# The eight-row sums of k and v: from a reduction on VectorE to three in-place additions on GpSimd

## Chip, core and metric

The kernel runs on one core of a Trainium2 chip. The metric is the device time of one execution in microseconds (us); the median of the executions is compared.

## What is computed

Attention over keys and values that are pooled by eight along the sequence, then two blocks of matrix products. The shapes are: batch 8, 8 heads, sequence 576, head size 64; 4608 tokens of width 512 afterwards.

```python
k_p = k.reshape(B, H, Sp, pool, D).mean(axis=3)      # pool = 8, Sp = 72
v_p = v.reshape(B, H, Sp, pool, D).mean(axis=3)
scores = scale * np.matmul(q, k_p.transpose(0, 1, 3, 2))
attn = softmax(scores)
x = np.matmul(attn, v_p)          # tokens x 512
h = ((x @ w1) * (x @ w2)) @ w3    # first block, width 1024
y = h @ w_out
r = np.maximum(y @ w_in, 0.0)     # second block, width 2048
out = (r * r) @ moe2_w_out
```

The change concerns the first two lines only: the sums over eight neighbouring rows of k and of v.

## The kernel before

The kernel computes w3 @ w_out once (the "fold": `fold`, L634, whose products are L754), so that the first block needs three products instead of four. While the fold runs, the attention of batches 0 and 1 runs between its steps; from about 119 us on the products of the first block take turns with the attention of the other batches, and from about 705 us on only the second block is left.

The weights come from DRAM as 64-bit words. For each 128x512 piece the SP queue loads `raw` (L130), ScalarE makes two passes (L136, L137), VectorE three (L145, L146 on `raw`, L148 on `w` or `wo`); TensorE transposes w3 (L696) or uses the piece as it is. A `raw` buffer is free again after L148, and only then can the next load of its ring start.

Per batch, k and v each are 576 pooled rows of 64 numbers, in five tiles: four of 128 rows and one of 64. A tile `kv` holds for each pooled row its eight source rows (128 x 8 x 64). `kv_parts` (L276 to L313) gives a list of steps: load a tile on the SP queue (L286, L288, L291), sum it (`total`, L296), and what follows. For k that is the copy of `kp` beside itself on GpSimd (L318, L319) and then TensorE's transposes (L353, L359). For v it is `cut`, which splits the sums into a high and a low part on VectorE (L328, L329), and `place`, which puts them in the operands `vl` and `vr` by 16 small DMAs on the SP queue (L334, L338). That makes ten sums per batch and 80 in all, each one instruction of VectorE.

Per tile of 128 queries the attention takes: scores on TensorE (L432), row maximum and its scaling on VectorE (L446, L447), exponentials on ScalarE (L449), the reciprocal sum on VectorE (L455, L456), then on GpSimd the product with it (L457) and two small copies (L461), then transposes on TensorE (L479, L484), a split into high and low parts on ScalarE and VectorE (L119, L120, L485, L487) and the product with v (L178, L497), whose result is split again (L510, L513). Five such tiles make one batch, 40 in all; they are called attention tiles here.

Each engine executes its instructions in one fixed order, and so does the SP queue. That order is settled when the program is built: the framework orders the instructions by its own estimate of when each can run, so that a change of one helper shifts neighbours as well.

Of the kernel before, what the change touches and what calls it, by code (L numbers as in the profile page):

```python
# [13 lines left out]
AX = mybir.AxisListType  # L14
# [3 lines left out]
POOL = 8  # L18
# [17 lines left out]
def attn_moe_moe2_kernel(  # L36
# [16 lines left out]
    nc = tc.nc  # L53
# [202 lines left out]
    def kv_rows(j):  # L256
        return P if j < NJ - 1 else JL
# [18 lines left out]
    def kv_parts(src, b, dst, last):  # L276

        flat = src[b].rearrange("h (s r) d -> (h s) r d", r=POOL)
        raws = {}

        def load(j):
            pool, tag = (raw_p, "raw") if b else (wW_p, "w")
            raws[j] = r = pool.tile([P, POOL, D], F32, tag=tag, name="kv")
            if src is k:
                n = kv_rows(j)
                nc.sync.dma_start(r[:n], flat[j * P:j * P + n])  # L286
            elif j < NP:
                nc.sync.dma_start(r, flat[j * 2 * SP:j * 2 * SP + P])  # L288
            else:
                for c in range(NP):  # L290
                    nc.sync.dma_start(  # L291
                        r[c * RM:(c + 1) * RM], flat[c * 2 * SP + P:(c + 1) * 2 * SP])

        def total(j):
            n = kv_rows(j)
            nc.vector.reduce_sum(  # L296
                dst(j)[:n], raws[j][:n].rearrange("p r d -> p d r"), axis=AX.X)

        def part(j):
            if j >= 2:  # L300
                total(j - 2)
            if j < NJ:
                load(j)

        if b == 0:
            fits = NJ if src is k else U1 - NJ
            for j in range(fits):
                load(j)
            rest = [lambda: [load(j) for j in range(fits, NJ)]]
            return rest + [(lambda j=j: total(j)) for j in range(NJ)] + last  # L310
        parts = [(lambda j=j: part(j)) for j in range(NJ + 2)] + last
        what = (src is k, b)
        back["kv"].extend((what, fn) for fn in parts)  # L313
# [1055 lines left out]
    for step in order:  # L1369
        if step[0] == "h":  # L1370
            _, p, u, n = step
# [61 lines left out]
```

## Time and profile before

| | us |
|---|---|
| median of 3 runs | 1554.29 |
| lowest and highest of them | 1553.34, 1557.86 |
| the profiled execution | 1549.5 |
| span of the profiled execution | 1547.7 |

The span runs from the first to the last instruction of the program. TensorE's matmuls are busy for 97% of it, VectorE for 64%, ScalarE for 50%, GpSimd for 5%. A share of the whole span is a mean over stages with different limits, so a table of stretches is read beside it, and the chain of work that ended last shows which engine each stretch hung on. A duration in such a row is that of the instruction as recorded, with what it waited inside the engine; a number in brackets is idle time ahead of it, and what ended that.

### The profile page before, as it was taken

To read this page: it belongs to the slowest core of one execution; us is meant where nothing else is said; L and a number is where in the kernel's file an instruction comes from. 1 tells how busy PE (TensorE), PEld (TensorE's weight loads), DVE (VectorE), ACT (ScalarE), POOL (GpSimd) and SP (SyncE) were. 2 spreads that over 40 slices of the span, in tenths; PEclk is the share of its full clock that TensorE was granted. 3 is DMA by queue.
4 is the path that set the end of the run, shared out by engine and by line. 5 is a ranking of instruction groups with operands and counts; after the bars stand their busy time and mean duration, and the time that the engine had idled before them with its cause. 6 is when DMAs were issued, how large, how long until landed. Compare 5 with 4: busy or idle time off the path is not lost.

```text
span 1547.7 us, 21838 instructions
## 1 busy us (share of the span) xinstructions
PE 1498.4 (97%) x6944; PEld 1204.2 (78%) x6944; DVE 989.7 (64%) x1778; ACT 780.7 (50%) x1905; POOL 82.1 (5%) x146
## 2 busy tenths in 40 slices
PE   5799999999999999999999999999999999999998
PEld 3457787877787787878887878887788778888888
DVE  7897675757565564767245477659665976576442
ACT  6766555444444444545134574456445644554431
POOL 1011111101010001100000000000000000000000
PEclk9999999999999999999999999999999999999999
DMA  9555656565564856667439777778777867776774
GB/s 297 185 155 153 169 169 179 161 186 154 171 189 137 261 151 178 186 222 242 117 127 310 202 204 231 206 207 230 222 207 207 231 195 206 207 222 191 212 223 150
DMA packets 300625, 303.86 MB, mean 196 GB/s; under 512 B 131296, under 2 KB 188640, under 8 KB 300512
## 3 DMA queue, kind: packets, MB, share of 16 engines
q1 hardware_dynamic: 295328, 293.04, 65.5%
q10 hardware_dynamic: 5184, 9.44, 1.7%
q8 instruction: 56, 0.92, 0.2%
q14 instruction: 57, 0.47, 0.1%
HBM read 243.27 MB, written 56.62 MB: 194 GB/s over the span
## 4 chain that ended last, share of the span: by engine, by line
PE 73%; DVE 12%; DMA 5%; ACT 4%; SPq 3%; issue 2%; DVEq 0%; ACTq 0%
PE ps_w L178 21%; PE o L1149 15%; PE acc L178 10%; PE ps_c L1062 5%; PE ps_d L1062 5%; PE ps_a L1062 5%; PE o L1209 3%; PE ps_h L178 3%; PE ps_b L1062 2%; DVE gs L1127 2%; PE ps_s L432 2%; DVE gt L120 2%; SPq L338 2%; DMA raw<-in_moe_w_dram 1%; PE ps_av L178 1%
## 5 line engine op out<-in xcount | busy, mean ns | idle before, releaser
L1149 PE MATMUL o<-gt,un 128*128 128x512 f32 x1344 | 330.9, 390 | 4.9 <-DVE gt L120 4.5
L1149 PEld LDWEIGHTS o<-gt,un 128*128 128x128 f32 x1344 | 251.6, 188 | 60.9 <-DVE gt L120 9.0
L120 DVE TENSOR_TENSOR gt<-gs,gt 128x512 fp32r<-128x512 f32 x240 | 164.2, 689 | 189.9 <-ACT gt L119 189.6
L178 PE MATMUL ps_w<-x,wt 128*128 128x512 f32 x960 | 249.9, 401 | 2.2 <-DVE x L513 1.1
L119 ACT CAST gt<-gs 128x512 fp32r<-128x512 f32 x240 | 148.5, 620 | 163.9 <-PE o L1149 111.2
L178 PE MATMUL acc<-gt,Wt 128*128 128x512 f32 x864 | 221.1, 397 | 1.3 <-ACT st L819 1.3
L178 PEld LDWEIGHTS ps_w<-x,wt 128*128 128x128 f32 x960 | 174.2, 189 | 39.1 <-DVE x L513 3.0
L178 PE MATMUL ps_w<-x,un 128*128 128x512 f32 x768 | 191.1, 396 | 2.1 <-DMA un<-u_w 2.1
L178 PEld LDWEIGHTS acc<-gt,Wt 128*128 128x128 f32 x864 | 158.8, 189 | 34.1 <-ACT st L819 1.8
L178 PEld LDWEIGHTS ps_w<-x,un 128*128 128x128 f32 x768 | 140.8, 188 | 30.8 <-ACT oq L872 1.8
L449 ACT ACTIVATE att<-ps_s,mx 128x72 f32<-128x72 f32 (+1 forms) x320 | 97.9, 321 | 64.0 <-DVE mx L447 59.7
L1069 ACT ACTIVATE r<-r 128x512 f32<-128x512 f32 x96 | 60.5, 631 | 113.0 <-DVE r L1099 112.3
L1062 PE MATMUL ps_a<-x2o,un 128*128 128x512 f32 x384 | 97.7, 390 | 1.6 <-ACT r L1069 1.6
L791 DVE TENSOR_TENSOR gf<-asb,ps_w 128x512 f32<-128x512 f32 x72 | 49.2, 684 | 77.5 <-PE ps_w L178 74.4
L1062 PE MATMUL ps_c<-x2o,un 128*128 128x512 f32 x384 | 97.9, 390 | 0.3 <-DVE u L1093 0.2
L1062 PE MATMUL ps_d<-x2o,un 128*128 128x512 f32 x384 | 97.5, 389 | 0.0
L1070 ACT ACTIVATE gs<-r 128x512 f32<-128x512 f32 x144 | 89.5, 628 | 1.6
L119 ACT CAST gt<-gf 128x512 fp32r<-128x512 f32 x72 | 44.8, 623 | 81.7 <-DVE gf L791 77.6
L1127 DVE TENSOR_TENSOR gs<-gs 128x512 f32<-128x512 f32 x128 | 83.9, 690 | 2.2 <-ACT gs L1070 0.9
L1062 PEld LDWEIGHTS ps_a<-x2o,un 128*128 128x128 f32 x384 | 72.0, 188 | 17.1 <-ACT r L1069 2.0
L1062 PEld LDWEIGHTS ps_c<-x2o,un 128*128 128x128 f32 x384 | 71.9, 188 | 16.3 <-DVE u L1093 1.5
L1062 PEld LDWEIGHTS ps_d<-x2o,un 128*128 128x128 f32 x384 | 72.1, 188 | 15.0
(109 smaller groups left out, 1957.3 us busy)
## 6 DMA issues: line engine op xcount, KB each, us to landing
un<-u_w SPq DMA_DIRECT2D x128, 256.0 KB
un<-u_A SPq DMA_DIRECT2D x128, 256.0 KB
un<-u_S SPq DMA_DIRECT2D x128, 256.0 KB
un<-u_oA SPq DMA_DIRECT2D x128, 256.0 KB
un<-u_oS SPq DMA_DIRECT2D x128, 256.0 KB
raw<-in_moe_w_dram SPq DMA_DIRECT2D x32, 512.0 KB
raw<-in_moe_w_out_dram SPq DMA_DIRECT2D x24, 512.0 KB
x2d<-st ACTq DMA_DIRECT2D x36, 256.0 KB
```

Of the source, the lines that this page charges most:

```text
L119: nc.scalar.copy(hi, src)
L120: (eng or nc.vector).tensor_sub(lo, src, f32(hi))
L178: (lambda a=a, b=b, i=i: nc.tensor.matmul(ps, a, b, start=first and i == 0, stop=last and i == n - 1))
L338: nc.sync.dma_start(f32(vr)[r0:r0 + RM, c, 1, :], vhl[c * RM:(c + 1) * RM, i // 2, NP, :])
L449: nc.scalar.activation(av[:, h0 + h], sv[:, h], ACTF.Exp, bias=mx[:n, h:h + 1], scale=scale, accum_out=sm[:n, h0 + h:h0 + h + 1])
L791: nc.vector.tensor_mul(gf, asb, pss[1])
L1062: nc.tensor.matmul(ps, l, r, start=first and j == 0, stop=j == len(todo) - 1, skip_group_check=True)
L1069: nc.scalar.activation(t, src, ACTF.Relu)
L1070: nc.scalar.activation(take(name), t, ACTF.Square)
L1127: nc.vector.tensor_sub(src, a, src)
L1149: nc.tensor.matmul(ob[x][o], l, r, start=u == 0 and m != 5 and j == 0, stop=u == NU - 1 and j == 2, skip_group_check=True)
L1209: nc.tensor.matmul(acc[o][:, y * PC:(y + 1) * PC], l, r, start=u == 0 and y == 0 and j == 0, stop=u == U2 - 1 and j == 2, skip_group_check ...
```

## The change

The sums of batch 0's k stay as they were. The other 75 sums are made on GpSimd, each by three additions: the upper four of the eight rows are added onto the lower four, in place in `kv` (128x256 numbers), then two onto two (128x128), then the last two into the destination (128x64). The second and third addition read what the one before wrote.

```diff
         def total(j):
             n = kv_rows(j)
-            nc.vector.reduce_sum(
-                dst(j)[:n], raws[j][:n].rearrange("p r d -> p d r"), axis=AX.X)
+            r = raws[j][:n]
+            if src is k and b == 0:
+                nc.vector.reduce_sum(dst(j)[:n], r.rearrange("p r d -> p d r"), axis=AX.X)
+                return
+            for w in (POOL // 2, POOL // 4):
+                nc.gpsimd.tensor_add(r[:, :w], r[:, :w], r[:, w:2 * w])
+            nc.gpsimd.tensor_add(dst(j)[:n], r[:, 0], r[:, 1])
```

Below this place all line numbers are larger by 5 in the changed kernel: L446 is L451 there, L457 is L462, and so on. Each row of the following lists is an instruction in its engine's order: line, operation, output, inputs, shape.

On GpSimd, before, from the copies of batch 0's k to the second attention tile:

```order
L318 COPY kp<-kp 128x4x64
L319 COPY kp<-kp 64x64
L457 TENSOR_TENSOR att_102<-att_102,sm 128x576
L461 COPY rem<-att_102 128x96 x2
L457 TENSOR_TENSOR att_103<-att_103,sm 128x576
L461 COPY rem<-att_103 128x96 x2
```

On GpSimd, with the change, the last of the three trees that stand between those copies and the first attention tile, and what follows it:

```order
L301 TENSOR_TENSOR kv<-kv 128x256
L301 TENSOR_TENSOR kv<-kv 128x128
L302 TENSOR_TENSOR vhl<-kv 128x64
L462 TENSOR_TENSOR att_102<-att_102,sm 128x576
L466 COPY rem<-att_102 128x96 x2
L462 TENSOR_TENSOR att_103<-att_103,sm 128x576
L466 COPY rem<-att_103 128x96 x2
```

Three trees of three additions for batch 0's v now stand ahead of the product of the first attention tile.

On VectorE, before, the last two sums of batch 0's v, up to its cut (L328, L329):

```order
L296 TENSOR_REDUCE vhl<-kv 128x64
L148 ISA w_419<-raw,w_419 128x1024
L145 TENSOR_SCALAR raw<-raw 128x512
L455 TENSOR_SCALAR sm<-sm 128x8
L146 SCALAR_TENSOR_TENSOR raw<-raw 128x2x256
L711 TENSOR_TENSOR wt<-w_419,wt 128x512
L148 ISA wo<-raw,wo 128x1024
L296 TENSOR_REDUCE vhl<-kv 64x64
L456 RECIPROCAL sm<-sm 128x8
L328 CAST vhl<-vhl 128x320
L329 TENSOR_TENSOR vhl<-vhl 128x320
```

On VectorE, with the change, the same place and what follows the cut (L333, L334 here):

```order
L716 TENSOR_TENSOR wt<-w_423,wt 128x512
L333 CAST vhl<-vhl 128x320
L334 TENSOR_TENSOR vhl<-vhl 128x320
L145 TENSOR_SCALAR raw<-raw 128x512
L146 SCALAR_TENSOR_TENSOR raw<-raw 128x2x256
L120 TENSOR_TENSOR Wt<-ps_w,Wt 128x512
L148 ISA w_457<-raw,w_457 128x1024
L145 TENSOR_SCALAR raw<-raw 128x512
L451 TENSOR_REDUCE mx<-ps_s 128x4
L146 SCALAR_TENSOR_TENSOR raw<-raw 128x2x256
```

The two sums are gone from ahead of the cut, and the row maxima of the third attention tile, which stood well ahead of the cut before (at L446, 13 rows above the first row of the list before), now come behind it, and with them that tile's reciprocal sum.

## Rows read from the trace of the kernel before

**Rows 1.** Page, part 1: engine, busy us (share of the span), instructions.

```profile
PE 1498.4 (97%) x6944; PEld 1204.2 (78%) x6944; DVE 989.7 (64%) x1778; ACT 780.7 (50%) x1905; POOL 82.1 (5%) x146
```

**Rows 2.** Stretches: length, busy us (instructions) by engine, TensorE clock, DMA share, GB/s.

```profile
17.00:70.00 53.00, 39.94 (x142) 20.12 (x141) 45.44 (x90) 39.19 (x108) 5.39 (x9) 0.98 0.64 206
70.00:119.00 49.00, 46.56 (x181) 26.10 (x180) 47.24 (x94) 33.53 (x98) 4.94 (x8) 0.96 0.59 186
119.00:705.00 586.00, 574.29 (x2762) 461.28 (x2763) 378.67 (x791) 291.27 (x982) 66.69 (x114) 1.00 0.62 179
705.00:1547.70 842.70, 831.40 (x3838) 691.64 (x3836) 509.19 (x792) 409.21 (x709) 1.61 (x3) 1.00 0.71 207
```

**Rows 3.** Chain that ended last, 17 to 66 us: start, length, what.

```profile
20.07 0.15 DVE vhl L296
20.22 0.79 issue
...
22.03 0.95 DVE vhl L296
...
45.55 0.07 DVE vhl L296
45.62 0.79 issue
...
49.37 0.93 DVE vhl L296
```

**Rows 4.** Timeline to 30 us: start, length, engine, line, what [idle before].

```profile
8.29 0.40 POOL L318 COPY kp<-kp 128x256 f32<-128x256 f32 x1 [4.85 <-DVE kp L296]
...
9.22 0.23 POOL L319 COPY kp<-kp 64x64 f32<-64x64 f32 x1 [0.54 <-DVE kp L296]
...
24.89 1.15 POOL L457 TENSOR_TENSOR att<-att,sm 128x576 f32<-128x576 f32 x1 [15.45 <-DVE mx L447]
```

**Rows 5.** Timeline, 81 to 98 us, GpSimd and VectorE.

```profile
81.83 1.15 POOL L457 TENSOR_TENSOR att<-att,sm 128x576 f32<-128x576 f32 x1 [27.71 <-DVE sm L456]
...
82.21 1.32 DVE L711 TENSOR_TENSOR wt<-w,wt 128x512 fp32r<-128x512 f32 x1
...
96.06 0.68 DVE L148 CUSTOM_DVE_ANT_0 w<-raw,w 128x1024 uint16<-128x1024 uint16 x1
96.19 0.80 POOL L318 COPY kp<-kp 128x256 f32<-128x256 f32 x1 [4.48 <-DVE kp L296]
```

**Rows 6.** Groups of VectorE, 17 to 119 us: busy, mean ns | idle before.

```profile
L146 DVE SCALAR_TENSOR_TENSOR raw<-raw 128x512 uint32<-128x512 uint32 x30 | 20.6, 687 | 0.3
L148 DVE CUSTOM_DVE_ANT_0 w<-raw,w 128x1024 uint16<-128x1024 uint16 x23 | 15.8, 686 | 0.2
L145 DVE TENSOR_SCALAR raw<-raw 128x512 uint32<-128x512 uint32 x30 | 12.7, 424 | 1.8 <-ACT w L137 1.4 <-ACT wo L137 0.3
L296 DVE TENSOR_REDUCE vhl<-kv 128x64 f32<-128x512 f32 (+1 forms) x10 | 10.2, 1032 | 0.0
L296 DVE TENSOR_REDUCE kp<-kv 128x64 f32<-128x512 f32 (+1 forms) x8 | 8.3, 1038 | 0.0
```

**Rows 7.** Timeline, 38 to 40 us, third attention tile on VectorE.

```profile
38.77 0.82 DVE L446 TENSOR_REDUCE mx<-ps_s 128x4 f32<-128x288 f32 x2
...
39.84 0.23 DVE L447 TENSOR_SCALAR mx<-mx 128x4 f32<-128x4 f32 x2
```

**Rows 8.** Timeline, 50 to 70 us, from the cut to the next loads.

```profile
50.72 3.94 SPq L334 DMA_DIRECT2D vl<-vhl  x4
...
54.77 7.56 SPq L338 DMA_DIRECT2D vr<-vhl  x12
...
62.43 4.82 SPq L130 DMA_DIRECT2D raw<-in_moe_w_dram  x8
...
69.54 0.80 PE L178 MATMUL ps_av<-aT,vl 128*128 128x256 f32 x2 [4.32 <-DVE x L513]
```

**Rows 9.** Line L457: who waited for it (us, times).

```profile
  PEld ps_t L479: 1.6, 2
```

## The prediction

> **What bounds the kernel now.** The page comes first: TensorE's matmuls are busy for 97% of the span, VectorE for 64%, GpSimd for 5% [rows 1]. That alone would say that work taken off VectorE is worth nothing, but the shares are means over stages. The table of stretches tells them apart [rows 2]. From 705 us on there is no sum of k or v any more, so nothing changes there. From 119 to 705 us TensorE is busy for 574.29 of 586 us; it idles 11.7 us and VectorE has a third of its time free, so this is TensorE's stretch. From 17 to 70 us it is the other way round: VectorE is busy for 45.44 of 53 us and TensorE for 39.94, so 13.1 us of TensorE's time are lost. From 70 to 119 us both are full: VectorE 47.24 of 49, TensorE 46.56, so only 2.4 us are lost there. The chain of waits agrees: up to 119 us it runs mostly through VectorE's passes over the weights and through the sums, after that through TensorE. Whatever the change gives, it gives in the first 119 us, and at most 15.5 us, the idle time of the two stretches.
>
> Of the sums, five lie between 17 and 70 us (batch 0's v), and 13 between 70 and 119 us (k and v of batch 1, three of batch 2's k): 18, at 1.03 us each [rows 6]. The other 57 that move lie in TensorE's stretch.
>
> **What is taken off VectorE.** A sum of 1.03 us stands in the chain with 0.86 to 0.95 us, since neighbours overlap by a little: four of the first five are in it, 0.15+0.79, 0.95, 0.07+0.79 and 0.93 (the "issue" behind a sum is its remainder) [rows 3]. The fifth doesn't stand in the chain, and I count it as nothing. So 3.7 us leave the chain before 50 us.
>
> **What GpSimd takes for it.** No row shows such an addition. The nearest is the product of an attention tile, also two inputs from SBUF: 1.15 us for 576 numbers per row [rows 4]. Two copies, 0.40 us for 256 numbers and 0.23 us for 64 [rows 4], make a fixed part of about 0.17 us. With it the product costs 1.7 ns a number, and a tree of 256+128+64 = 448 numbers is 3 x 0.17 + 0.76 = 1.27 us; without it, in proportion, 0.90 us. I take 1.27, because the copy of 64 numbers plainly doesn't shrink in proportion. 75 trees are 68 to 95 us on an engine that has 82 us of work in 1548 [rows 1]; GpSimd becomes no bound. Nor is the later end of a single sum a matter: GpSimd has idled 27.7 us before one product and 4.5 us before a copy [rows 5], so a tree begins when its load lands, while the sum waited its turn on VectorE.
>
> **What the trees do to VectorE.** This decides. While GpSimd made a product at 81.83 us, a subtraction of VectorE that reads two tiles from SBUF (L711) took 1.32 us [rows 5]; L146, of the same 128x512 and also with two inputs from SBUF, takes 0.69 us [rows 6]. In the other direction a copy of `kp` that started 0.13 us into VectorE's L148 took 0.80 us [rows 5], not 0.40 [rows 4]. The two engines exclude each other there. L145, L146 and L148, all on SBUF alone, fill 49.1 us from 17 to 119 us [rows 6], two thirds of the 74 us that VectorE is busy there without the sums (45.44 + 47.24 [rows 2] less 10.2 + 8.3); the rest reads mostly PSUM. So a tree can be paid for twice. Lower bound of its price to VectorE: nothing, where VectorE idles or reads PSUM. Upper bound: its whole 1.27 us, more than the sum cost. I take the part that grows with the numbers, 0.76 us, times two thirds to four fifths: 0.55 us. The fixed part, I assume, passes beside VectorE, as in the disturbed copy: VectorE ended at 96.74 us and the copy 0.25 us later, well under its 0.40. A tree is then a gain of 0.4 us of VectorE's time (bounds: -0.3 and +0.95).
>
> 17 to 70 us: 3.7 us leave the chain, five trees put back 5 x 0.55 = 2.8; gain 0.9 us. The order adds something. The row maxima of the third attention tile stood ahead of the cut of batch 0's v, 1.05 us [rows 7], and its reciprocal sum beside it; all of it now comes behind the cut. The cut matters: after it 16 small DMAs hold the SP queue from 50.72 to 62.33 us, eight loads of weights stand behind them from 62.43 us, and TensorE idles 4.32 us up to 69.54 us for want of them [rows 8]. A cut that is earlier moves all this forward, and what was moved behind it falls into the hole: 1.1 us. Together 2.0 us.
>
> 70 to 119 us: 13 trees free 13 x 0.4 = 5.2 us of VectorE, but TensorE can give back only its 2.4 us of idle time; I take half, 1.2 us.
>
> 119 to 705 us: 57 us leave VectorE, which isn't late there; the price is that a product waits behind trees on GpSimd, and a subtraction ahead of a matmul behind a tree. TensorE's weight loads have waited for the products 1.6 us in all [rows 9]. I take nothing, with 3 us to either side, as the framework also orders TensorE's steps anew all over this stretch.
>
> Sum: 2.0 + 1.2 + 0 = 3.2 us. The profiled execution took 1549.5 us and would take 1546.3. It lies 4.8 us under the median of the runs, 1554.29; against that, 1551 us.
>
> **The rivals.**
>
> *VectorE gains the whole sums* (faster). Between 17 and 119 us the trees fall beside L446, L513 and the other readers of PSUM, or into idle time. For it: GpSimd has nothing else to do, and the trees for batch 0's v can run while the weights' loads still fill the DMA queues. Then 3.7+1.1 us before 70 us and the 2.4 us after it: 1547 us; with the hole of 4.32 us closed as well, 1543 us. Against it: two thirds of VectorE's work collides.
>
> *The port costs more than the sums did* (slower). VectorE is full from 17 to 119 us, so every tree meets an instruction of its kind; if each addition stops it for its full length, a tree costs 1.27 us and saves 0.95: 18 x 0.32 = 5.8 us more, 1560 us. It decides as soon as more than three quarters of a tree's length is lost on VectorE. For it: L711 lost 0.63 us to the last 0.77 us of one product [rows 5, 6]. Against it: the fixed part, and that in the second stretch TensorE's queue is as full. The Trainium skill, in "SBUF — State Buffer", section "Who interferes with whom", states this rule: a GpSimd instruction that reads SBUF and a VectorE instruction with two SBUF inputs exclude each other for the whole instruction, whereas a reduction of VectorE never contends. By that rule the change swaps work that disturbs nobody for work that does; the trace agrees on L711 (1.32 us, where 0.69 us is usual) and shows no tree.
>
> *A tree that waits for its load holds an attention tile's product behind it on GpSimd* (slower). GpSimd takes its list in order, and TensorE takes its own in order as well. A product that is used at once is late by one tree, 1.27 us; eight such tiles out of 35 would cost 10 us, less the 3.2: 1561 us. Against it: only two waits of the weight loads on L457 in the whole trace, 1.6 us [rows 9], so nearly all products are early enough.
>
> **How the numbers follow.** A measurement of this kernel can tell 0.3%, 4.7 us, from no change. The forecast, a gain of 3 us that stays within that: 0.53. The first rival, in the part of it that passes 4.7 us: 0.31. The port: 0.10. The held products: 0.06. So faster 0.31, same 0.53, slower 0.16. The range goes from 1545 us, the first rival with a part of the hole closed, to 1559 us, just short of the two slower ones; some 0.1 is left out on either side.
>
> **What the profile of the changed kernel would show.** The busy time of VectorE falls by about 75 x 1.05 = 79 us, less 20 to 40 us by which L145, L146, L148, L711 and the subtractions that read SBUF become longer; their means from 17 to 119 us tell the price of the port directly (0.69 us before for L146 and L148). A tree takes 1.3 us in its three rows when undisturbed. The 16 small DMAs begin 1 to 3 us before 50.72 us, and the products of the first block begin that much earlier. If L146 and L148 keep 0.69 us, the first rival holds; if their means pass 0.9 us, the second. TensorE's idle time from 119 to 705 us stays near 11.7 us; if it grows beyond 17 us with L479 waiting for L462, it is the third. I would be wrong altogether if the second block's time changed.

## The result, and the profile after

The change is slower. The changed kernel takes 1571.24 us (median of 6 runs, 1567.93 to 1573.06), the kernel before 1553.39 us in the same comparison (6 runs, 1551.81 to 1557.86): a ratio of 1.0116, 95% interval 1.0099 to 1.0133, some 18 us. The forecast was 1551 us with a range of 1545 to 1559; the result lies 12 us above it. The profiled execution after has a span of 1571.0 us, where the one before had 1547.7: these two lie 23.3 us apart, 5 more than the medians, since the execution profiled before (1549.5 us) was quicker than any of the six and the one after (1572.78 us) slower than most.

Lines of the kernel after stand 5 further down (L457 became L462, L479 became L484); a tree is L301 twice and, for its last addition, L302.

First the page's part 1, as in [rows 1]: engine, busy us, share, instructions.

```profile
PE 1506.2 (96%) x6944; PEld 1209.7 (77%) x6944; DVE 935.0 (60%) x1703; ACT 783.3 (50%) x1905; POOL 213.0 (14%) x371
```

VectorE got what it was to get: it is busy for 54.7 us less. The span grew by 23.3 us all the same, and the row splits that: TensorE idles 15.5 us more (1571.0 - 1506.2 = 64.8 us, against 1547.7 - 1498.4 = 49.3), and is busy for 7.8 us more with the same 6944 matmuls. The second part is its clock. The mean granted clock fell from 0.996 to 0.990 (before, then after):

```profile
core 0: 1547.7 us, clock 0.996
...
core 0: 1571.0 us, clock 0.990
```

With two levels, 2.4 and 1.2 GHz, that is some 31 us at the lower one (2 x 0.010 x 1571), where before it was 12; 19 us more at half speed would be about 9 us of lost work if TensorE were busy throughout; for a part of that time it is idle.

Now the stretches of [rows 2], in the kernel after (length, then busy us and instructions of PE, PEld, DVE, ACT and POOL, TensorE's clock, DMA share, GB/s).

```profile
17.00:70.00 53.00, 41.18 (x142) 20.56 (x140) 43.32 (x82) 37.47 (x104) 16.14 (x24) 0.97 0.62 199
70.00:119.00 49.00, 39.58 (x146) 23.05 (x147) 41.12 (x80) 32.69 (x93) 30.71 (x46) 0.86 0.60 188
119.00:705.00 586.00, 566.59 (x2691) 453.03 (x2690) 314.63 (x695) 279.95 (x935) 158.84 (x284) 0.99 0.60 168
705.00:1571.00 866.00, 853.18 (x3946) 708.29 (x3944) 527.17 (x834) 426.21 (x764) 3.79 (x6) 1.00 0.72 209
```

From 70 to 119 us TensorE idles 9.4 us (2.4 before) and its clock is 0.86 (0.96 before). From 119 to 705 us it idles 19.4 us (11.7 before). GpSimd, which had 4.94 us of work from 70 to 119 us, has 30.71 there. After that nothing is added: what the kernel before does from 829 us on stands 23.2 us later here, right to the end.

What TensorE waits for is new too. This is, as in [rows 9], who waited for the product of an attention tile (line L462: us, times). TensorE's matmuls waited 9.4 us, where it was 0.5; its weight loads, which stand ahead of the same matmuls, waited 10.7 us in the same two gaps, where it was 1.6.

```profile
  PEld ps_t L484: 10.7, 2
  PE ps_t L484: 9.4, 2
  PEld ps_t L489: 0.7, 2
```

The 9.4 us are two gaps; of the 15.5 us by which TensorE's idle time grew, the other 6 have other causes. The first gap, in the timeline of GpSimd, VectorE and TensorE (start us, us, engine, line, what, [idle before <- whom it waited for]):

```profile
94.07 0.18 DVE L461 RECIPROCAL sm<-sm 64x8 f32<-64x8 f32 x1
...
79.86 1.37 POOL L301 TENSOR_TENSOR kv<-kv 128x256 f32<-128x256 f32 x2 [12.19 <-DMA kv<-in_k_dram]
...
91.18 2.35 POOL L323 COPY kp<-kp 128x256 f32<-128x256 f32 x1
93.50 1.25 POOL L301 TENSOR_TENSOR kv<-kv 64x256 f32<-64x256 f32 x2
94.83 0.77 POOL L302 TENSOR_TENSOR kp<-kv 64x64 f32<-64x64 f32 x1
95.67 0.58 POOL L324 COPY kp<-kp 64x64 f32<-64x64 f32 x1
96.21 1.32 POOL L301 TENSOR_TENSOR kv<-kv 128x256 f32<-128x256 f32 x2
97.61 0.65 POOL L302 TENSOR_TENSOR vhl<-kv 128x64 f32<-128x64 f32 x1
98.22 1.25 POOL L301 TENSOR_TENSOR kv<-kv 128x256 f32<-128x256 f32 x2
99.54 0.32 POOL L302 TENSOR_TENSOR vhl<-kv 128x64 f32<-128x64 f32 x1
99.82 1.14 POOL L462 TENSOR_TENSOR att<-att,sm 64x576 f32<-64x576 f32 x1
...
101.02 0.69 PE L484 MATMUL ps_t<-ident,att 64*128 64x64 f32 x4 [6.00 <-POOL att L462]
```

The reciprocal sum, the product's last input, is there at 94.25 us. GpSimd doesn't idle; it works through the rest of batch 1's k and two trees of its v, which stand ahead in its queue, and starts the product 5.56 us later.

The length of this train comes in part from VectorE's work on SBUF beside it. From 79.86 us, when the rows of batch 1's k land after 12.19 us of idle time, GpSimd works without a break up to the product at 99.82 us: seven trees, the product of tile 3 and the copies, 20 us in all. The copy of `kp` takes 2.35 us there, where it took 0.40 [rows 4]. At the undisturbed lengths (1.6 us from the start of a tree to what follows it at 98.22 us) the same work would take some 14 us, an estimate; the 6 us of difference are as much as the product's wait.

TensorE stands still for 6.00 us, and then runs slowly (the windows 95.00 to 101.10 and 101.10 to 107.00 us, columns as above; the clock is the third figure from the end):

```profile
95.00:101.10 6.10, 0.10 (x2) 0.09 (x2) 3.07 (x4) 1.23 (x3) 5.66 (x10) 0.78 0.94 233
101.10:107.00 5.90, 5.90 (x23) 3.98 (x24) 3.42 (x6) 3.29 (x9) 3.89 (x7) 0.64 0.43 141
```

The second gap begins with a wait for a load:

```profile
131.56 1.28 POOL L301 TENSOR_TENSOR kv<-kv 128x256 f32<-128x256 f32 x2 [11.90 <-DMA kv<-in_k_dram]
132.92 0.32 POOL L302 TENSOR_TENSOR kp<-kv 128x64 f32<-128x64 f32 x1
133.31 0.40 POOL L323 COPY kp<-kp 128x256 f32<-128x256 f32 x1
133.66 1.25 POOL L301 TENSOR_TENSOR kv<-kv 64x256 f32<-64x256 f32 x2
134.99 0.31 POOL L302 TENSOR_TENSOR kp<-kv 64x64 f32<-64x64 f32 x1
135.37 0.23 POOL L324 COPY kp<-kp 64x64 f32<-64x64 f32 x1
135.56 1.14 POOL L462 TENSOR_TENSOR att<-att,sm 128x576 f32<-128x576 f32 x1
...
136.75 1.12 PE L484 MATMUL ps_t<-ident,att 128*128 128x128 f32 x4 [3.42 <-POOL att L462]
```

GpSimd idles 11.90 us in front of a tree whose rows of k haven't landed, while a product whose inputs are there at 129.94 us, and the next one's at 133.17 us, stand behind it. Of the 5.62 us that the first of them waits, 1.6 are the rest of that load; the other 4 are the two trees and the copies behind it. Of the 40 products, four wait for 3.9 to 5.6 us (tiles 4, 5, 6 and 22, counted from 0); before, none waited over 0.5 us.

### The profile page after: what moved, and what is told of

Same layout as the page of the kernel before. It is cut to its first block, busy times and chain, and to the rows that moved or that the text cites. A ratio compares the mean times of both kernels' runs of the same rounds, so it can differ in the third digit from the quotient of the medians.

```text
span 1571.0 us, 22041 instructions
## 1 busy us (share of the span) xinstructions
PE 1506.2 (96%) x6944; PEld 1209.7 (77%) x6944; DVE 935.0 (60%) x1703; ACT 783.3 (50%) x1905; POOL 213.0 (14%) x371
## 4 chain that ended last, share of the span: by engine, by line
PE 72%; DVE 9%; DMA 6%; ACT 4%; SPq 3%; POOL 3%; issue 2%; DVEq 0%; POOLq 0%; ACTq 0%
PE ps_w L178 19%; PE o L1154 14%; PE acc L178 9%; PE ps_a L1067 5%; PE ps_c L1067 5%; PE ps_d L1067 5%; PE o L1214 3%; PE ps_h L178 3%; PE ps_w L759 2%; PE ps_b L1067 2%; DVE gs L1132 2%; PE ps_s L437 2%; DVE gt L120 2%; POOL kv L301 2%; DMA raw<-in_moe_w_out_dram 2%
## 5 line engine op out<-in xcount | busy, mean ns | idle before, releaser
L178 PE MATMUL ps_w<-x,wt 128*128 128x512 f32 x960 | 253.4, 405 | 5.6 <-ACT asb L792 3.8
L301 POOL TENSOR_TENSOR kv<-kv 128x256 f32<-128x256 f32 (+3 forms) x150 | 101.0, 674 | 94.4 <-DMA kv<-in_v_dram 48.6
L796 DVE TENSOR_TENSOR gf<-asb,ps_w 128x512 f32<-128x512 f32 x72 | 49.3, 685 | 98.7 <-PE ps_w L178 93.3
L462 POOL TENSOR_TENSOR att<-att,sm 128x576 f32<-128x576 f32 (+1 forms) x40 | 48.8, 1219 | 346.6 <-DVE sm L461 196.0
```

The costliest lines, as they stand in the source:

```text
L178: (lambda a=a, b=b, i=i: nc.tensor.matmul(ps, a, b, start=first and i == 0, stop=last and i == n - 1))
L301: nc.gpsimd.tensor_add(r[:, :w], r[:, :w], r[:, w:2 * w])
L462: nc.gpsimd.tensor_mul(av, av, sm[:n].unsqueeze(2).to_broadcast([n, H, SP]))
L796: nc.vector.tensor_mul(gf, asb, pss[1])
```

## The experiments

The theories: **Q**, finished products wait on GpSimd behind trees. **P**, the two engines hinder each other on SBUF. **S** (formed after the first four runs), the head of the program is put in another order. **R**, the framework's new order on all engines, an accident with no one cause. Ratios are to the kernel before, with 95% intervals.

### Where the loss arises

**e3, e4.** Trees for only a part of the batches; the rest of the sums stays on VectorE. The condition under which `total` uses VectorE:

```diff
-            if src is k and b == 0:
+            if b > 1 or src is k and b == 0:      # e3_early_only
+            if b < 2:                             # e4_late_only
```

> Trees only for batch 0's v and batch 1's k and v (15 of 75); all later sums are VectorE's as before. By the shift of the milestones in the changed kernel (+10.8 us at 100, +14.5 at 172, +25 at the most, later), the theories that put the loss into the head (Q with its first two gaps, or P with the join at 17 to 60) expect +9 to +14 us: 1563 to 1568. If the loss comes from a creep over all batches, under +5 us: below 1558.

> Trees only for batches 2 to 7 (60 of 75); the head is as before. The rest of the loss by the same shifts: +8 to +12 us if stages add up (1561 to 1566), through GpSimd's backlogs at 131 and at 385 to 408. If the head alone carries the loss: within 3 us of the kernel before, 1551 to 1556.

Measured: e3 1566.69 us, 1.0097 (1.0079 to 1.0114); e4 1558.81 us, 1.0044 (1.0027 to 1.0060). The 15 early trees cost 14 us, the 60 later ones 6 or 7, which lies between the two ranges expected for e4. e3 keeps the gap at 96 us, 7.04 us long there. e4 has neither of the two gaps shown above; its longest one between 17 and 705 us, after that at 66 us which the kernel before has too, is a late cut of v (TensorE waits for the transfers that place v):

```profile
399.86 0.77 PE L178 MATMUL ps_av<-aT,vl 128*128 128x256 f32 x2 [3.65 <-DMA vl<-vhl]
```

A product waits behind trees in e4 too, that of tile 22, for 2.61 us.

**e6, e7.** The early 15, divided once more: batch 0's v alone (5 trees), and batch 1's k and v alone (10 trees).

```diff
-            if src is k and b == 0:
+            if src is k or b > 0:                 # e6_v0_only
+            if b != 1:                            # e7_batch1_only
```

> Only batch 0's five v sums are trees on GpSimd (5 of 75); k and v of all later batches stay with VectorE. No tree is left beside the products of tiles 3 to 6. Theory Q: nothing waits behind trees, so only the join at 17 to 50 us counts (+3 to +4 us): 1555 to 1557. Theory S: the head is rearranged as in the changed kernel, the jump at 90 to 97 us is still there, half or more of it: 1558 to 1564.

> Only batch 1's k and v sums are trees on GpSimd (10 of 75); batch 0's v and all later sums are VectorE's. The head up to 75 us is in the order of the kernel before. Theory Q: products 3 and 4 wait behind these trees as in the changed kernel: +6 to +9 us, 1558 to 1562. Theory S: the jump at 90 to 97 us does not come: 1552 to 1556.

Measured: e6 1554.7 us, 1.0013 (1.0001 to 1.0025); e7 1569.6 us, 1.0103 (1.0068 to 1.0139). Ten trees of 75 make nearly the whole loss, more than any theory had for them. Their gap (e7, TensorE, then two windows around it):

```profile
100.66 0.68 PE L484 MATMUL ps_t<-ident,att 64*128 64x64 f32 x4 [7.05 <-POOL att L462]
```

```profile
93.60:100.60 7.00, 0.01 (x1) 0.00 (x0) 3.55 (x5) 1.32 (x3) 6.47 (x11) 0.74 0.97 261
100.60:108.00 7.40, 7.34 (x23) 4.95 (x24) 3.40 (x8) 3.70 (x9) 3.26 (x8) 0.55 0.56 163
```

The product here is ready at 93.18 us and starts at 99.46. Seven microseconds of stillness and another seven at nearly half speed: one wait costs some 10 us (7.05 idle, and 7.34 busy at 0.55, which is 3.3 of lost work). The 5 trees of batch 0's v, which meet no waiting product, cost 2 us. The parts don't add up to the whole: 2 + 16 + 6 or 7 us against 18.

Nor does the wait explain all of e7. Here are the products of the fold and the program's last products, before and in e7 (line, count, ns min/median/max, start of the first and of the last in us):

```profile
L754 PE MATMUL ps_w<-wo,w3t x128: 590/593/1220, 16.7 to 116.2; 128*128 128x512 f32 x128
L759 PE MATMUL ps_w<-wo,w3t x128: 590/592/1221, 17.3 to 126.5; 128*128 128x512 f32 x128
...
L1209 PE MATMUL o<-un,gt x384: 278/283/284, 1497.0 to 1542.9; 128*128 128x256 f32 x192
L1214 PE MATMUL o<-un,gt x384: 278/283/284, 1519.3 to 1565.2; 128*128 128x256 f32 x192
```

The fold ends 10.3 us late, and the program 22.3 us late in these two executions. The other 12 us arise after the fold, where e7 has no tree left and the framework's order differs; what makes them is not shown.

### Is it the place of the third tile (S)?

**e5, e8.** Priority to the scores of batch 0's second and third tile (e5), or of all tiles but the first (e8), over the preparation of weights.

```diff
     def pe_s(g, half):
+        if g in (1, 2):                           # e8: if g >= 1
+            with tc.high_priority(offset=400):
+                pe_s_now(g, half)
+        else:
+            pe_s_now(g, half)
+
+    def pe_s_now(g, half):
```

> The changed kernel with one thing altered: the scores of batch 0's second and third attention tile (matrix products, maxima, exponentials, sums, product) are given priority over the preparation of weights, so that the third tile's maxima stand on VectorE ahead of v's cut again, as in the kernel before; in the changed kernel they stand behind it and that tile's product starts at 65.6 us where it started at 50.6. Trees and their engine are unchanged. Theory S (the rearranged head: the third tile comes 15 us later, so the fourth and fifth are squeezed against batch 1's loads and trees): the fold's shift at 97 us falls from +10.8 to +3 to +5, the time to 1563 to 1566. Theory Q (finished products behind trees, which this leaves where they are): 1569 to 1573.

> The changed kernel with the priority of e5 for the scores of every attention tile but the first. By the order of the instructions the products of tiles 4 to 6 then stand ahead of the trees that they waited for, and the third tile's maxima ahead of the cut. If Q and S together make the loss, the time comes to within 5 us of the kernel before: 1551 to 1558. If what is left is the two engines' contention for SBUF or the trees' own length, it stays above 1562.

Measured: e5 1573.72 us, 1.0126 (1.0095 to 1.0157); e8 1567.57 us, 1.0099 (1.0067 to 1.0132). The maxima came ahead of the cut again and the third tile's product at 40 us, 10 us earlier than in the kernel before; nothing was gained. S falls. In e8 the waits were not removed but moved: the products of tiles 4 and 6 still waited 5.76 and 6.59 us, so that e8 doesn't tell what would be left without them.

### Is it GpSimd's order (Q)?

**e1, e9.** The changed kernel with edges that fix only the order of issue on GpSimd: named trees behind named products and the small copies that follow these (abridged).

```diff
+    for tree, g in TREE_AFTER:                    # (is k, batch, tile of rows), product
+        tc.add_manual_dep(firsts[tree].ins, prods[g].ins.name, NoSync, reason="order")
...
+TREE_AFTER = [((False, 1, j), 4) for j in range(5)] + [((True, 2, 3), 5),
+    ((True, 2, 4), 6)] + [((False, 4, j), 22) for j in range(1, 5)]     # e1
+    + [((True, 1, 2), 3), ((True, 1, 3), 4), ((True, 1, 4), 4)]         # e9, besides
```

> The changed kernel with one thing altered: on GpSimd, the trees that stood ahead of four finished products of attention (the products of tiles 4, 5, 6 and 22, which waited 5.56, 5.62, 4.02 and 3.86 us with all their inputs ready) are issued behind those products. No instruction is added or taken away. Theory Q (GpSimd's one queue: finished products wait behind trees): the four waits fall below 1.5 us each, the gaps of 6.00 us at 95 and 3.42 us at 133 on TensorE shrink to under 2.5 and 1.5, the half-clock stretches behind them go, and the time falls by 8 to 14 us, to 1557 to 1563. Theory P (the two engines hinder each other on SBUF, VectorE is slowed): nothing of that kind changes, 1568 to 1573. Theory R (the time is in the framework's other order on all engines, an accident): some other value, up or down, with no link to those gaps.

> The changed kernel with GpSimd's order altered further than in e1_order: of batch 1's k, the last three trees, and all of v's, are issued behind the products of tiles 3 and 4 (e1 left k's trees ahead of them, and these products still waited 4.07 and 4.61 us there); tiles 5, 6 and 22 as in e1. No instruction is added. Theory Q (products behind trees, and the half clock that follows the gap on TensorE): products 3 and 4 wait under 1 us, the gap of 4.2 us at 94 goes, the stretch from 17 to 125 us loses another 3 to 6 us, time 1555 to 1560. If the trees cost by their contention for SBUF with VectorE or by late loads, the time stays where e1 had it, 1560 to 1565, with the gap under another name (a weight load or the copy of aR).

Measured: e1 1562.47 us, 1.0072 (1.0057 to 1.0087); e9 1565.31 us, 1.0073 (1.0051 to 1.0094). By the ratios, order alone gives back some 7 of the 18 us, so Q is right in kind, but neither run does all that was expected of it: e1's time lies at the upper end of Q's range, e9's 5 us above it. In e1 the gap at 95 us shrank to 4.23 us, since trees of k still stood ahead. In e9 it is gone: tile 4's product starts as soon as its sum is there. But the next products wait instead:

```profile
95.21 1.14 POOL L469 TENSOR_TENSOR att<-att,sm 64x576 f32<-64x576 f32 x1 [3.92 <-DVE sm L468]
...
129.93 1.25 POOL L307 TENSOR_TENSOR kv<-kv 128x256 f32<-128x256 f32 x2 [11.90 <-DMA kv<-in_k_dram]
131.15 1.15 POOL L469 TENSOR_TENSOR att<-att,sm 128x576 f32<-128x576 f32 x1
...
135.55 1.15 POOL L469 TENSOR_TENSOR att<-att,sm 128x576 f32<-128x576 f32 x1
```

Tiles 5 and 6 (L469 here) waited 5.03 and 6.20 us. Ahead of tile 5 stands a tree that no edge names, and 3.8 of the 5.03 us are the end of its wait for a load; the tree that was put behind tile 5 now stands ahead of tile 6. Turned about on one queue, the collision moves.

### Trees without products on their engine

**e2, e11, e12.** The product and its two copies on VectorE, in the kernel after (e2), in the kernel before as a control (e11), and in e4 (e12).

```diff
-        nc.gpsimd.tensor_mul(av, av, sm[:n].unsqueeze(2).to_broadcast([n, H, SP]))
+        nc.vector.tensor_mul(av, av, sm[:n].unsqueeze(2).to_broadcast([n, H, SP]))
...
-            nc.gpsimd.tensor_copy(
+            nc.vector.tensor_copy(
```

> The changed kernel with the product of attention and its two small copies made by VectorE, so that only sums and the copies of k are left on GpSimd. Theory Q: TensorE's transposes wait no longer for a product behind trees; the gap at 95 falls from 6.00 to under 2.5 us; VectorE gains about 40 x 1 us of work beside 79 us of sums that it lost, so the time comes to 1553 to 1560. Theory P: VectorE stays slowed by the trees and has 40 us more to do: 1571 to 1580.

> The kernel before (all sums on VectorE) with the product of attention and its two small copies made by VectorE: the control for e2, which differs from it only by the 75 trees on GpSimd. VectorE has some 32 us more to do than in the kernel before. If what the trees cost is that products wait behind them (Q), a kernel without products on GpSimd has nothing to lose: e2's 1556.5 is then the price of the product's move, and this control comes to 1554 to 1558. If the trees themselves cost (contention, late loads), the control is near the kernel before, 1551 to 1554, and e2's 4 us are theirs.

> e4_late_only (trees for batches 2 to 7 alone, 1558.8) with the product and its copies on VectorE, so that no product stands behind a tree. Theory Q: the 6.5 us of e4 fall to what the control e11 has, within 2 us of it. If the late trees cost by late sums (v's cut and its transfers behind a backlog of trees, as the gap of 3.65 us at 396 in e4 suggests) or by contention, it stays 4 to 7 us above e11.

Measured: e2 1556.49 us, 1.0029 (1.0011 to 1.0046); e11 1557.67 us, 1.0029 (1.0015 to 1.0043); e12 1556.72 us, 1.0024 (1.0010 to 1.0038). With all 75 trees on GpSimd (e2) and with none (e11) the time is the same: the difference is 0 with an uncertainty of some 3.5 us (the two intervals combined), against 18 us when the product stands on GpSimd too. The late trees alone (e12) cost nothing either. So the loss needs both, trees and products, on GpSimd. The 0.3% is there without any tree (e11), as the price of VectorE's new work and of the order that comes with it. In e2 TensorE waits for the product (line L462, on VectorE) once, for 0.7 us:

```profile
  PE ps_t L484: 0.7, 1
```

What this leaves open: e2 holds VectorE's relief and its hindrance at once, and shows only that their sum is near nothing. The gap at 95 us was to fall below 2.5 us in e2; one of 3.25 us stands there, which hangs not on a product but on a load of weights that was issued at 94.77 us, behind loads of v:

```profile
101.40 0.63 PE L502 MATMUL ps_av<-aR,vr 96*128 96x320 f32 x1 [3.25 <-DVE aR L492]
```

From 70 to 119 us TensorE's clock is 0.86 in e2, as in the changed kernel, and in its profiled execution (1561.63 us, 5 above its median) the fold ends at 124.1 us, in e11's at 117.6. The trees are thus not free in the head even there; of these two executions, e11's loses 8 us on the kernel before after the fold, e2's 4. The two controls also don't part the queue from the two engines' hindrance on SBUF: with the product on VectorE it matters no longer how long a train of trees is. And in e4 the longest wait named above was for a late cut, not for a product; that e12 loses nothing shows that the products are needed for that loss, but not by which of the waits.

### The same trees on VectorE

**e10.** All 80 sums as three in-place additions on VectorE, GpSimd as before; the diff is against the changed kernel.

```diff
-            if src is k and b == 0:
-                nc.vector.reduce_sum(dst(j)[:n], r.rearrange("p r d -> p d r"), axis=AX.X)
-                return
-                nc.gpsimd.tensor_add(r[:, :w], r[:, :w], r[:, w:2 * w])
-            nc.gpsimd.tensor_add(dst(j)[:n], r[:, 0], r[:, 1])
+                nc.vector.tensor_add(r[:, :w], r[:, :w], r[:, w:2 * w])
+            nc.vector.tensor_add(dst(j)[:n], r[:, 0], r[:, 1])
```

> The same three in-place additions, for all 80 sums, but on VectorE; GpSimd keeps the products and copies of the kernel before. From GpSimd's rows the tree is long there (0.72, 0.45 and 0.32 us undisturbed); on VectorE no run shows it yet: the additions of 128x512 (0.60 us) give some 0.35, 0.2 and 0.12 us as an estimate, against 1.03 us for the reduction that it replaces, so that VectorE has 20 to 30 us less to do. If the tree as such or the framework's new order makes the loss (theory R), this is slower than the kernel before too, above 1558. If the loss comes with GpSimd (Q, or contention), it is at or below the kernel before, 1545 to 1554.

Measured: 1550.13 us, 0.9980 (0.9964 to 0.9996): the tree as such, with the framework's new order that comes with it, doesn't cost. R in its plain form, that any order which comes with the tree costs, falls. But each version has an order of its own, and the 12 us of e7 that arise where it has no tree remain open. e10 is the one version that is not behind the kernel before: it is ahead by 0.04 to 0.36%. The estimate for it was too low, though. The groups on VectorE (busy us, mean ns of one):

```profile
L298 DVE TENSOR_TENSOR kv<-kv 128x256 f32<-128x256 f32 x64 | 27.8, 438 | 14.0 <-DMA kv<-in_k_dram 11.5 <-DMA kv<-in_v_dram 2.5
L298 DVE TENSOR_TENSOR kv<-kv 128x128 f32<-128x128 f32 x64 | 18.9, 298 | 0.8
L299 DVE TENSOR_TENSOR vhl<-kv 128x64 f32<-128x64 f32 x32 | 7.3, 235 | 0.4
```

0.44 + 0.30 + 0.23 = 0.97 us in place of 1.03 us [rows 6]; VectorE's busy time fell by 13.7 us (989.7 to 976.0), since neighbours overlap, not by 20 to 30.

## Why the prediction was wrong

**The term for a product that waits behind trees.** This is the step that failed. In the sum it stands at nothing: from 119 to 705 us by "I take nothing, with 3 us to either side", and from 70 to 119 us there is no such term at all, where the first and longest wait came (6.00 us of idle TensorE and a clock of 0.64 behind it; the changed kernel ends its fold at 125.8 us, 9.6 late). The reason given was that a tree begins when its load lands and that GpSimd is idle; but the loads of batch 1's k land close together, after 12.19 us of idle time, and the trees then run as one train. For the stretch from 119 to 705 us the prediction named its own test, TensorE's idle time beyond 17 us with the transposes waiting for the product, and it came out: 19.4 us, with L484 waiting for L462, though that wait is 3.42 of the 7.7 us by which the idle time grew. The third rival, held at 0.06, is the mechanism that happened, with the difference that the product waits mostly for trees and little for their loads.

**The rival's price.** It counted one tree per late product, 1.27 us, eight times. What was measured is four products with 3.9 to 5.6 us each. The size was wrong for three reasons: the framework put several trees in a row ahead of one product, VectorE's work made the additions longer (by some 6 us in the first train, the estimate above), and a gap of that length on TensorE is followed by a stretch at the lower clock that costs 2 to 3 us more. [Rows 9] were read the wrong way round: that products had been early enough in an engine that idled 27.7 us before one of them [rows 5] says nothing about an engine that is busy for 30.71 of 49 us.

**70 to 119 us: a gain of 1.2.** It became 7 us more of idle time and a clock of 0.86; e7 (39.20 us busy of 49, a clock of 0.83) shows that batch 1's ten trees do this.

**17 to 70 us: a gain of 2.0.** The sign was wrong, by little. The 16 small DMAs were to start 1 to 3 us before 50.72 us [rows 8]; they start later:

```profile
52.93 3.71 SPq L339 DMA_DIRECT2D vl<-vhl  x4
```

e6 has these five trees alone and loses 1.8 us (0.2 to 3.9). Of the 2.0, 1.1 us were to come from the third tile's maxima behind the cut; e5 put them back ahead of it and lost nothing measurable by that.

**What the trees cost VectorE.** This step held, with a price somewhat too high. L146, L148 and L145 from 17 to 119 us, as in [rows 6]:

```profile
L146 DVE SCALAR_TENSOR_TENSOR raw<-raw 128x512 uint32<-128x512 uint32 x30 | 21.7, 724 | 0.3
L148 DVE CUSTOM_DVE_ANT_0 w<-raw,w 128x1024 uint16<-128x1024 uint16 x23 | 18.3, 794 | 0.1
L145 DVE TENSOR_SCALAR raw<-raw 128x512 uint32<-128x512 uint32 x30 | 16.4, 546 | 2.7 <-ACT w L137 2.0 <-ACT wo L137 0.7
```

They grew by 1.1 + 2.5 + 3.7 = 7.3 us, 0.4 us for each of the 17 trees that end in that window here (0.55 was forecast for all of VectorE's work), and their means stay under the 0.9 us at which the second rival would have held. VectorE's whole busy time fell by 54.7 us: 79 less 24, inside the 20 to 40 that were to be given back, or 0.3 us for each of the 75 trees.

**The tree's own length.** 1.27 us was the larger of its two prices. Undisturbed it is 1.25 us for the two large additions and 0.32 for the last, 1.6 us with the gap between them, and neither price held a disturbed one: the prediction priced the two engines' hindrance on VectorE alone. GpSimd pays too (below), and its length is what sets how long a product waits.

**The first rival** (VectorE gains the whole sums) had 0.31. VectorE did gain some of them, and e2 beside e11, where VectorE is busy for 967.2 and 1019.2 us and the time is the same, shows no use of such a gain; as e2 also has the trees' hindrance in it, it doesn't price the gain alone.

## What to carry to other kernels

When work goes to an idle engine, look first at what that engine already does for the engine that sets the time. Its small, urgent steps now stand in order behind long trains of work that can wait, and behind that work's loads; the price of one is the whole train, not one piece of it, at the lengths that the pieces have beside the other engines. A control that moves the urgent step elsewhere in both versions (e2 against e11) shows in two runs whether the loss hangs on that meeting; it doesn't show what made the train long. And mending the order by hand at the places that show it may only move the collision to the next place.

## What the runs showed of the hardware

**A gap on TensorE costs more than its length.** The gaps of 6 and 7 us above were each followed by a stretch in which TensorE was busy throughout at a mean clock of 0.64 and 0.55: 2.1 us (5.90 x 0.36) and 3.3 us of lost work behind them. Not every difference in the clock is the change's: e6's profiled execution has 49.4 us of idle TensorE, as before, and 5.0 us more busy at a mean clock of 0.993, but the kernel before was itself granted 0.993 to 0.998 from one execution to the next. The Trainium skill, "TensorE: Matmul & The Clock Gate", section "HAM oscillation — how this bites in real kernels", prices time at the lower clock at half its length; by that the 19 us more of it here would be 9.5 us, an estimate; the trace agrees roughly, TensorE's busy time grew by 7.8 us.

**SBUF is shared in both directions.** Two additions of a tree took 1.25 us at 98.22 us (above), where VectorE was idle, and 3.39 us in e7 where it was busy without a break. Each has its window (busy us in the order PE, PEld, DVE, ACT, POOL); between them is GpSimd's row of e7:

```profile
98.22:99.47 1.25, 0.00 (x0) 0.00 (x0) 0.00 (x0) 0.00 (x0) 1.17 (x3) 0.60 0.90 155
```

```profile
89.06 3.39 POOL L301 TENSOR_TENSOR kv<-kv 128x256 f32<-128x256 f32 x2
```

```profile
89.06:92.45 3.39, 3.39 (x16) 1.65 (x15) 3.39 (x9) 3.33 (x18) 3.31 (x3) 1.00 0.16 54
```

The Trainium skill states this in "SBUF — State Buffer", section "Who interferes with whom": whichever of the two engines holds the shared ports keeps them for its whole instruction, and the other stands still. The trace agrees: L146 and L148 keep their usual 0.68 us in that window of e7, and GpSimd's pair of short additions takes nearly three times as long.
